# Keys and values of two batches turned at once, and scores as products of array halves, in a fused attention and expert kernel

## The chip, the core and the metric

The kernel runs on one core of a Trainium2 chip. The core has five engines that work side by side, each through its own list of instructions in order, and that meet through semaphores: TensorE (PE) for matrix products, VectorE (DVE) and ScalarE (ACT) for elementwise work, GpSimd (POOL), and SyncE (SP), which here only starts transfers. A PE product needs its stationary operand loaded into the array first; the profile lists these loads apart, as PEld. PE writes only to PSUM, which DVE and ACT read. Other data lie in SBUF, whose 128 partitions are the rows of every tile.

The metric is the time of one execution on the device in microseconds (us); lower is better.

## The reference

Attention with pooled keys and values, and then a mixture of experts that takes one expert for each row:

```python
batch, n_heads, seq, head_dim = (8, 8, 576, 64)      # q, k, v
k_p = k.reshape(B, H, Sp, pool, D).mean(axis=3)      # pool = 8, Sp = 72
v_p = v.reshape(B, H, Sp, pool, D).mean(axis=3)
scores = scale * np.matmul(q, k_p.transpose(0, 1, 3, 2))
attn = exp(scores - max) / sum
x = np.matmul(attn, v_p)                             # rows: 4608 x 512
# experts: argmax of x @ w_gate, at most `capacity` rows for each of 8,
# relu(x @ w1) @ w2, times the row's gate probability
```

## The kernel before

The attention stage takes the first 210 us or so of the span, the experts the rest. The change touches the attention stage alone.

**Pooling.** Batches go in pairs, p = 0 to 3. The 576 rows of k and v of a pair come in as three transfers each (`raw`, `load_third`), with (batch, head, group) on the 128 partitions: partition (b h g) holds the nine pooled rows of one group. GpSimd adds eight rows to one in a tree of three additions (`tree`, L348 to L352) into `kps[p]` and `vps[p]`, [128, 9, 64]. For pair 0 VectorE helps.

**Turning.** The pooled rows have to stand with head_dim on the partitions. `turned` (L374) does this for one batch b and one of k and v: five products with the pooled tile as the stationary operand and the 64 columns of the identity that pick batch b as the moving one, into one PSUM bank `pk` (L382). The first four take two pooled rows of 64 together, 128 columns; the fifth the ninth row alone, 64 columns. `natural` (L387) copies them out on ACT in two copies (even and odd rows, L391). For keys, `prep_k` does this twice, into `kbs[b % 2]`, [128, 2, 8 heads, 72]: partitions 0 to 63 get the keys in half 0, partitions 64 to 127 the same keys in half 1, and the other two quarters stay zero from the start. For values, `prep_v` copies once, and then multiplies with `wgi` (identity and gate weights, L409) into the bank `pv`, which VectorE spreads to `vbd` (L411, L413).

**Units.** The queries of a batch are done in units of 256 rows and four heads; units of a pair number nine (j = 0 to 8, with n = 9p + j): four of the even batch, one `tail` that holds the last 64 rows of both batches (j = 4), and four of the odd batch. `q_part` transposes two row blocks of one head together (L433), so that partitions 0 to 63 of `qT` hold the one block and 64 to 127 the other. `score` (L436) then multiplies `qT[:, h]`, stationary, with the 144 columns of `kbs` for that head: because of the zeros, one product over 128 rows gives the 72 scores of either block (L448). In a tail unit the stationary operand is the 64 columns of one batch, so that products come in pairs that fill the two column halves of the array (L445).

**Order.** It is written out by hand in the loop over n. PE's share of a step is: half of the scores of unit n (`score(0)`), half of the transposes of the probabilities of unit n - 2 (`p_t(0)`, L471), the other halves of both, the queries of unit n + 1 (L433), then the products with the values of unit n - 2 (`av`, L485). PSUM banks for all of PE's transposes are taken in turn from two (`bank`). `hooks(n)` at the end of a step adds the turning: `prep_k` of the odd batch at j = 1 and of the next pair's even batch at j = 5, `prep_v` at j = 2 and j = 6 with its second part (the product with `wgi`) one step later. SP runs the transfers of queries, keys and values in the order of the program.

An f32 product of the program is two load and product pairs in the trace, a transpose is one pair: `score` of two heads shows as x4, `av` as x12, `turned` as x10 (eight with 128 columns, two with 64).

Of the kernel before, what the change touches and what calls it, by code (L numbers as in the profile page):

```python
# [10 lines left out]
F32 = mybir.dt.float32  # L11
# [20 lines left out]
def pooled_attn_top1_moe(ctx: ExitStack, tc: tile.TileContext, q, k, v, wg, w1, w2, cap, out):  # L32
# [125 lines left out]
    with ExitStack() as actx:  # L158
# [85 lines left out]
        kbs = [ac.tile([P, 2, H, SP_], F32, name=f"kbs{i}") for i in range(2)]  # L244
# [6 lines left out]
        nc.vector.memset(kbs[0], 0.0)  # L251
# [122 lines left out]
        def turned(x, b, w):  # L374

            while left.get((w, b // 2)):
# [9 lines left out]
        def natural(dst, pk):  # L386

            v = dst.rearrange("d h (g r) -> d (h g) r", r=NR)
            for o in range(2):
                n = (NR + 1 - o) // 2  # L390
                nc.scalar.copy(v[:, :, o : NR : 2], pk[o * D : (o + 1) * D, 0 : n * GB].rearrange("d (i q) -> d q i", q=GB))  # L391

        def prep_k(b):

            ks = kbs[b % 2]
            pk = turned(kps[b // 2], b, "k")
            for x in range(2):
                natural(ks[x * D : (x + 1) * D, x], pk)

        def prep_v(b):  # L400

            vT = wk.tile([D, H, SP_], F32, name="vT", tag="vT", bufs=1)
            natural(vT, turned(vps[b // 2], b, "v"))
            yield
            vb = vbd[b % 2]
            rows_ = vT.rearrange("d h x -> d (h x)")
# [7 lines left out]
            yield  # L414

        class Unit:
# [19 lines left out]
            def score(self, part):  # L436
                if part == 0:
                    self.ps = psc.tile([P, HH, 256], F32, name="ps", tag="ps")
# [12 lines left out]
            def softmax(self):  # L451

                sv = self.ps[:, :, 0 : 2 * SP_].rearrange("p h (a x) -> p h a x", a=2)
# [220 lines left out]
        rq, hq, aq, dq, sq, gq = [], [], [], [], [], []  # L674
# [42 lines left out]
        with tc.manual_schedule():  # L717
            nc.gpsimd.memset(kbs[1], 0.0)
# [502 lines left out]
```

## Time and profile before

| | us |
|---|---|
| median of 3 runs | 669.99 (669.15 to 671.27) |
| profiled execution, its own time | 671.99 |
| its span, first to last instruction | 669.8 |
| PE busy, of the span | 625.5 (93%) |
| mean granted PE clock | 0.981 |

The profile is one execution; times in it count from the first instruction. A row of the order of time reads: start, length of the merged group (from its first start to its last end), engine, line, operation, tiles, shapes, count, and in brackets the idle time ahead of it with what ended it. Ends of PE products are modelled and overlap the next, so the distance from one row's start to the next row's start is the time that a group took. In shapes, 128*64 is the array's part used, rows by columns.

### The profile page before, as it was taken

To read this page: it belongs to the slowest core of one execution; us is meant where nothing else is said; L and a number is where in the kernel's file an instruction comes from. 1 tells how busy PE (TensorE), PEld (TensorE's weight loads), DVE (VectorE), ACT (ScalarE), POOL (GpSimd) and SP (SyncE) were. 2 spreads that over 40 slices of the span, in tenths; PEclk is the share of its full clock that TensorE was granted. 3 is DMA by queue.
4 is the path that set the end of the run, shared out by engine and by line. 5 is a ranking of instruction groups with operands and counts; after the bars stand their busy time and mean duration, and the time that the engine had idled before them with its cause. 6 is when DMAs were issued, how large, how long until landed. Compare 5 with 4: busy or idle time off the path is not lost. (4 is left out here: it accounts for less than half of the span.)

```text
span 669.8 us, 14743 instructions
## 1 busy us (share of the span) xinstructions
PE 625.5 (93%) x4218; PEld 560.6 (84%) x4219; DVE 343.9 (51%) x783; ACT 236.8 (35%) x401; POOL 310.6 (46%) x467
## 2 busy tenths in 40 slices
PE   2899989999878989999999999999999999999994
PEld 2899879888777878997888899897998978989983
DVE  4466767778778832227826642224622466221222
ACT  2455545556454111215616431124311463111111
POOL 7699952543386323135543444313543056431444
PEclk9799989999899989999999999999999999999998
DMA  9994844344273151014843761101711181110112
GB/s 326 372 385 138 322 158 127 126 155 145 81 244 120 47 192 31 31 63 171 325 152 142 252 253 63 31 31 63 289 63 31 35 300 38 63 31 31 63 47 64
DMA packets 47086, 93.82 MB, mean 140 GB/s; under 512 B 13392, under 2 KB 23632, under 8 KB 47060
## 3 DMA queue, kind: packets, MB, share of 16 engines
q1 hardware_dynamic: 30836, 60.37, 25.9%
q0 software_dynamic: 11392, 21.57, 9.8%
q10 hardware_dynamic: 4832, 11.56, 4.5%
q8 instruction: 13, 0.21, 0.1%
q14 instruction: 13, 0.11, 0.1%
HBM read 132.97 MB, written 31.27 MB: 245 GB/s over the span
## 5 line engine op out<-in xcount | busy, mean ns | idle before, releaser
L1132 ACT ACTIVATE hh<-ph 128x512 fp32r<-128x512 f32 x60 | 35.9, 599 | 181.3 <-PE ph L146 169.7
L1133 DVE SCALAR_TENSOR_TENSOR hl<-ph,hh 128x512 fp32r<-128x512 f32 x60 | 41.0, 691 | 110.8 <-ACT hh L1132 47.6
L146 PE MATMUL ph<-xl,w1h 128*128 128x256 f32 x480 | 76.8, 282 | 2.6 <-DVE io L86 2.6
L146 PE MATMUL ph<-xh,w1h 128*128 128x256 f32 x480 | 76.9, 282 | 2.1 <-DVEq L1158 2.1
L146 PE MATMUL ph<-xh,w1l 128*128 128x256 f32 x480 | 76.5, 281 | 0.0
L155 PE MATMUL y<-w2h,hh 128*128 128x512 f32 x280 | 72.3, 400 | 0.0
L155 PE MATMUL y<-w2h,hl 128*128 128x512 f32 x280 | 71.0, 396 | 0.0
L155 PE MATMUL y<-w2l,hh 128*128 128x512 f32 x280 | 71.0, 396 | 0.0
L146 PEld LDWEIGHTS ph<-xh,w1h 128*128 128x128 f32 x480 | 66.7, 190 | 3.8 <-issue 2.5
L91 POOL DMA_INDIRECT xg<-xs,ix x42 | 41.1, 978 | 61.8 <-PE y L155 52.3
L146 PEld LDWEIGHTS ph<-xl,w1h 128*128 128x128 f32 x480 | 65.4, 189 | 3.3 <-issue 3.3
L146 PEld LDWEIGHTS ph<-xh,w1l 128*128 128x128 f32 x480 | 65.5, 190 | 0.0
L485 PE MATMUL pa<-vbd,pT 96*128 96x146 f32 (+1 forms) x480 | 63.1, 296 | 1.7 <-DVE lt L511 1.5
L155 PEld LDWEIGHTS y<-w2h,hl 128*128 128x128 f32 x280 | 52.6, 188 | 12.7
L155 PEld LDWEIGHTS y<-w2l,hh 128*128 128x128 f32 x280 | 52.6, 188 | 12.7
L89 POOL TENSOR_TENSOR guard<-ix 128x4 int32<-128x4 int32 x21 | 4.1, 197 | 122.6 <-DVE ix L86 77.5
L485 PEld LDWEIGHTS pa<-vbd,pT 96*128 96x128 f32 (+1 forms) x480 | 58.0, 186 | 3.0 <-ACT pT L472 2.4
L155 PEld LDWEIGHTS y<-w2h,hh 128*128 128x128 f32 x280 | 50.0, 188 | 9.4
L1153 DVE TENSOR_SCALAR ys<-y,io 128x512 f32<-128x512 f32 x40 | 30.0, 751 | 48.9 <-PE y L155 43.7
L122 DVE TENSOR_TENSOR xl<-px,xh 128x512 fp32r<-128x512 f32 x40 | 25.7, 685 | 56.4 <-ACT xh L121 56.4
L96 POOL DMA_INDIRECT out_dram<-zrow,iz x40 | 47.4, 1184 | 14.8 <-issue 13.6
L472 ACT COPY pT<-pp 96x384 f32<-96x384 f32 x72 | 33.9, 475 | 45.3 <-PE pp L471 44.2
(256 smaller groups left out, 1095.0 us busy)
## 6 DMA issues: line engine op xcount, KB each, us to landing
r<-in_moe_w_dram SPq DMA_DIRECT2D x84, 1024.0 KB, 10.9
raw<-in_k_dram SPq DMA_DIRECT2D x12, 768.0 KB, 7.4
raw<-in_v_dram SPq DMA_DIRECT2D x12, 768.0 KB, 9.4
xs<-xo ACTq DMA_DIRECT2D x16, 512.0 KB, 2.8
qblk<-in_q_dram SPq DMA_DIRECT2D x14, 512.0 KB, 6.0
raw<-in_moe_w_dram SPq DMA_DIRECT2D x4, 512.0 KB, 5.2
r<-in_moe_w_dram ACTq DMA_DIRECT2D x2, 1024.0 KB, 8.5
qblk<-in_q_dram SPq DMA_DIRECT2D x4, 256.0 KB, 8.1
```

What stands on the lines that cost most here:

```text
L89: nc.gpsimd.tensor_sub(guard, ix, ix)
L91: nc.gpsimd.indirect_dma_start(out=dst[:, i, :].bitcast(F32), out_offset=None, in_=src, in_offset=bass.IndirectOffsetOnAxis(ap=ix[:, i, 0: ...
L96: ins = nc.gpsimd.indirect_dma_start(out=out[:, :], out_offset=bass.IndirectOffsetOnAxis(ap=i_, axis=0), in_=src, in_offset=None, bounds_c ...
L122: eng.tensor_sub(lo, src, hi.bitcast(F32))
L146: nc.tensor.matmul(p[:, f2], a[:, c, f * P : (f + 1) * P], b[:, c], start=(f2 == 0 and j == 0 and c == 0), stop=(f2 == 1 and j == 2 and c ...
L155: nc.tensor.matmul(y, a[:, c, i * P : (i + 1) * P], b[:, c], start=(n == 0), stop=(n == 3 * KF - 1))
L472: nc.scalar.copy(self.pT[:, j], pp[0:KC, 0:HC])
L485: nc.tensor.matmul(self.pa[us, j, h0 * XW : (h0 + 2) * XW], self.pT[:, j, c, us], vbd[b % 2][:, cc].rearrange("r a x -> r (a x)"), start=( ...
L1132: nc.scalar.activation(hh[s], p, AF.Relu)
L1133: nc.vector.scalar_tensor_tensor(out=hl[s], in0=p, scalar=0.0, in1=hh[s].bitcast(F32), op0=ALU.max, op1=ALU.subtract)
L1153: nc.vector.tensor_scalar_mul(ys[i], y[i], io[:, i, 1:2].bitcast(F32))
```

## The change

`turned` now handles both batches of a pair, with five PE transposes (the whole 128-column identity moving): four into bank `pk`, the ninth row into a second bank `pl`. Three ACT copies take them out: two of 64x512, one of 64x128. Keys go to `kTp[p % 2]`, [128, 16 heads, 72]: partitions 0 to 63 are copied by ACT, and partitions 64 to 127 are a copy of them by a transfer on SP's queue (for pair 0 by three more ACT copies). Values go to `vTp`. The zeros are gone, with the two fills that made them.

`score` issues, for each head, two products over 64 rows each, of 72 columns: rows 0 to 63 of `qT` with rows 0 to 63 of `kTp` into one PSUM bank, rows 64 to 127 into the next. In a tail unit it is four products of 64 rows and 64 columns of the array.

In the hooks, the keys of the next pair are turned at j = 4, its values at j = 5, and the products with `wgi` come at j = 2 and j = 7, in one piece.

```diff
-        def turned(x, b, w):
+        def turned(dst, x, w, p):
...
-            pk = bank([P, 512], "pk")
-            bs = slice((b % 2) * GB, (b % 2 + 1) * GB)
-            for i in range(0, NR, 2):
-                m = min(2, NR - i) * D
-                nc.tensor.matmul(pk[0:m, i // 2 * GB : (i // 2 + 1) * GB], x[:, i : min(i + 2, NR)].rearrange("p r d -> p (r d)"),
-                                 ident[:, bs], start=True, stop=True)
-            return pk
...
+            pk, pl = bank([P, 4, P], "pk"), bank([P, 512], "pl")
+            for i in range(NR // 2):
+                nc.tensor.transpose(pk[:, i], x[:, 2 * i : 2 * i + 2].rearrange("p r d -> p (r d)"), ident)
+            nc.tensor.transpose(pl[0:D, 0:P], x[:, NR - 1], ident)
+            for t in dst:
+                v = t.rearrange("d h (g r) -> d (h g) r", r=NR)
+                for o in range(2):
+                    nc.scalar.copy(v[:, :, o : NR - 1 : 2], pk[o * D : (o + 1) * D].rearrange("d i q -> d q i"))
+                nc.scalar.copy(v[:, :, NR - 1 :], pl[0:D, 0:P, None])
+
+        def prep_k(p):
+            kt = kTp[p % 2]
+            if p:
+                turned([kt[0:D]], kps[p], "k", p)
+                nc.sync.dma_start(kt[D:], kt[0:D])
+            else:
+                turned([kt[0:D], kt[D:]], kps[p], "k", p)
...
-                    if self.tail:
-                        for u, b in enumerate(self.bs):
-                            us = slice(u * TAIL, (u + 1) * TAIL)
-
-                            two = kbs[b % 2].rearrange("p a h x -> p (a h) x")[:, h : h + H + HH + 1 : H + HH]
-                            nc.tensor.matmul(self.ps[us, h, 0 : 2 * SP_].rearrange("p (a x) -> p a x", a=2), self.qT[:, h, us], two,
-                                             start=True, stop=True)
-                    else:
-                        nc.tensor.matmul(self.ps[:, h, 0 : 2 * SP_].rearrange("p (a x) -> p a x", a=2), self.qT[:, h],
-                                         kbs[self.b % 2][:, :, self.hf * HH + h], start=True, stop=True)
+                    x = slice(h * SP_, (h + 1) * SP_)
+                    for u, b in enumerate(self.bs):
+                        us = slice(u * TAIL, (u + 1) * TAIL) if self.tail else slice(0, P)
+                        for a in range(2):
+                            rs = slice(a * D, (a + 1) * D)
+                            hd = (b % 2) * H + h + HH * (a if self.tail else self.hf)
+                            nc.tensor.matmul(self.ps[us, a, x], self.qT[rs, h, us], kTp[b // 2 % 2][rs, hd], start=True, stop=True)
...
                 elif n == 1:
-                    hq.append(prep_v(0))
-                    drain(hq)
+                    turned([vTp], vps[0], "v", 0)
+                    prep_v(0)
                 if p == B // 2:
                     return
-                if j == 1:
-                    prep_k(2 * p + 1)
                 if j == 2:
-                    hq.append(prep_v(2 * p + 1))
+                    prep_v(2 * p + 1)
                 if p + 1 < B // 2:
+                    if j == 4:
+                        prep_k(p + 1)
                     if j == 5:
-                        prep_k(2 * p + 2)
-                    if j == 6:
-                        hq.append(prep_v(2 * p + 2))
+                        turned([vTp], vps[p + 1], "v", p + 1)
+                    if j == 7:
+                        prep_v(2 * p + 2)
```

**PE, before, in the second pair, from the products with the values of step j = 1 on.** Rows are line, operation, output and inputs, the output's partitions x columns, and how many of the program's instructions stand in a row (`kbs_143` and `vbd_146` are tile names with their numbers).

```order
L485 MATMUL pa<-vbd_146,pT 128x146 x6
L382 MATMUL pk<-identr,kp 128x64 x4
L382 MATMUL pk<-identr,kp 64x64
L448 MATMUL ps<-kbs_143,qT 128x144 x2
L471 MATMUL pp<-identr,pt 96x128 x3
L448 MATMUL ps<-kbs_143,qT 128x144 x2
L471 MATMUL pp<-identr,pt 96x128 x3
L433 MATMUL pq<-identr,qblk 128x128 x4
```

**PE, after, at j = 4 of the first pair,** where the keys of both batches of the second pair are turned:

```order
L475 MATMUL pa<-vbd_146,pT 128x146 x6
L380 MATMUL pk<-identr,kp 128x128 x4
L381 MATMUL pl<-identr,kp 64x128
L439 MATMUL ps<-kTp_143,qT 128x72 x4
L461 MATMUL pp<-identr,pt 96x128 x3
L439 MATMUL ps<-kTp_143,qT 128x72 x4
L461 MATMUL pp<-identr,pt 96x128 x3
L425 MATMUL pq<-identr,qblk 128x128 x4
```

The turning keeps its five instructions, but there is one such place for a pair where there were two; each group of scores has twice the instructions, each with half of the columns.

**PE, after, where the product with `wgi` stands ahead of scores,** at j = 7 of the second pair:

```order
L475 MATMUL pa<-vbd_147,pT 128x146 x6
L402 MATMUL pv<-wgi,vTp 96x80 x6
L439 MATMUL ps<-kTp_144,qT 128x72 x4
L461 MATMUL pp<-identr,pt 96x128 x3
L439 MATMUL ps<-kTp_144,qT 128x72 x4
```

Like the scores behind it, the product with `wgi` uses 64 rows of the array.

**SP, the transfers of the first pair's time.** Before:

```order
L204 DMA qblk<-in_q_dram 128x4x256 x2
L187 DMA raw<-in_k_dram 128x1536 x3
L187 DMA raw<-in_v_dram 128x1536 x3
L204 DMA qblk<-in_q_dram 128x4x256 x2
L212 DMA qtail<-in_q_dram 64x4x64 x4
```

After:

```order
L204 DMA qblk<-in_q_dram 128x4x256 x2
L392 DMA kTp_144<-kTp_144 64x1152
L187 DMA raw<-in_k_dram 128x1536 x3
L187 DMA raw<-in_v_dram 128x1536 x3
L204 DMA qblk<-in_q_dram 128x4x256 x2
L212 DMA qtail<-in_q_dram 64x4x64 x4
```

The copy of the keys to the lower partitions stands ahead of the loads of the third pair's keys and values.

## Rows read from the trace of the kernel before

**Rows 1.** Busy time of each engine in stretches of 20 us of the attention stage, with the granted PE clock: the stretch, its length, then busy us and instructions of PE, PEld, DVE, ACT and POOL, the clock as a share of full speed, the busy share of the DMA engines, GB/s.

```profile
100.00:120.00 20.00, 20.00 (x166) 19.06 (x165) 14.41 (x45) 11.13 (x22) 5.95 (x10) 1.00 0.35 107
160.00:180.00 20.00, 15.96 (x134) 14.25 (x133) 16.45 (x51) 11.61 (x25) 9.64 (x9) 0.99 0.17 54
```

**Rows 2.** What PE waited for from 16 to 240 us: total us, times, longest.

```profile
PE pp L471 <- DVE vbd L413: 4.0, 2, 2.0
...
PE pp L471 <- ACT kbs L391: 1.9, 6, 0.3
PE pq L433 <- ACT pT L472: 1.8, 2, 1.1
```

**Rows 3.** PE in order of time: one step without turning, and the start of the next.

```profile
63.11 0.65 PE L448 MATMUL ps<-kbs,qT 128*128 128x144 f32 x4
63.60 0.49 PE L471 MATMUL pp<-identr,pt 128*96 128x128 f32 x3
63.93 0.66 PE L448 MATMUL ps<-kbs,qT 128*128 128x144 f32 x4
...
64.75 0.62 PE L433 MATMUL pq<-identr,qblk 128*128 128x128 f32 x4
65.20 1.66 PE L485 MATMUL pa<-vbd,pT 96*128 96x146 f32 x12
66.70 0.66 PE L448 MATMUL ps<-kbs,qT 128*128 128x144 f32 x4
```

**Rows 4.** PE in order of time: a turning of keys, the step behind it, a turning of values, and the start of what follows its step.

```profile
70.29 1.26 PE L382 MATMUL pk<-identr,kp 128*128 128x64 f32 x10
71.48 0.76 PE L448 MATMUL ps<-kbs,qT 128*128 128x144 f32 x4
...
73.39 0.53 PE L471 MATMUL pp<-identr,pt 128*96 128x128 f32 x3 [0.33 <-ACT kbs L391]
...
75.88 1.26 PE L382 MATMUL pk<-identr,vp 128*128 128x64 f32 x10
...
80.86 1.24 PE L409 MATMUL pv<-wgi,vT 64*96 64x80 f32 x12
```

**Rows 5.** PE in order of time: full-row products, the product with `wgi` on 64 rows, full-row products again.

```profile
103.55 1.66 PE L485 MATMUL pa<-vbd,pT 96*128 96x146 f32 x12
105.14 1.24 PE L409 MATMUL pv<-wgi,vT 64*96 64x80 f32 x12
106.31 0.76 PE L448 MATMUL ps<-kbs,qT 128*128 128x144 f32 x4
106.91 0.49 PE L471 MATMUL pp<-identr,pt 128*96 128x128 f32 x3
```

**Rows 6.** PE in order of time: scores of a tail unit, on two column halves.

```profile
129.00 0.71 PE L445 MATMUL ps<-kbs,qT 128*64 128x144 f32 x8
129.64 0.53 PE L471 MATMUL pp<-identr,pt 128*96 128x128 f32 x3
130.10 0.71 PE L445 MATMUL ps<-kbs,qT 128*64 128x144 f32 x8
```

**Rows 7.** PE in order of time: the router's counts, products of 8 columns that each load 128 columns, and the turning behind them.

```profile
99.64 0.37 PE L604 MATMUL po<-su,rlow 128*128 128x8 f32 x2
99.86 0.37 PE L604 MATMUL po<-su,chigh 128*128 128x8 f32 x2
100.08 1.34 PE L382 MATMUL pk<-identr,vp 128*128 128x64 f32 x10
```

**Rows 8.** ACT's copies out of PSUM from 16 to 240 us, by shape: count, busy us, mean ns of one, idle ahead.

```profile
L434 ACT COPY qT<-pq 128x512 f32<-128x512 f32 x36 | 21.1, 586 | 7.6 <-PE pq L433 6.7
L391 ACT COPY kbs<-pk 64x320 f32<-64x320 f32 x14 | 6.1, 437 | 8.8 <-PE pk L382 8.7
L391 ACT COPY kbs<-pk 64x256 f32<-64x256 f32 x14 | 5.8, 414 | 0.2
```

**Rows 9.** PE in order of time, at the start.

```profile
16.05 2.29 PE L448 MATMUL ps<-kbs,qT 128*128 128x144 f32 x8 [1.38 <-ACT qT L434]
...
24.21 1.24 PE L409 MATMUL pv<-wgi,vT 64*96 64x80 f32 x12 [1.56 <-ACT vT L391]
25.38 1.96 PE L382 MATMUL pk<-identr,kp 128*128 128x64 f32 x10
27.27 1.33 PE L448 MATMUL ps<-kbs,qT 128*128 128x144 f32 x4
```

**Rows 10.** PE in order of time, in the fourth batch pair's first steps.

```profile
163.60 0.53 PE L471 MATMUL pp<-identr,pt 128*96 128x128 f32 x3 [0.32 <-ACT kbs L391]
165.26 0.66 PE L433 MATMUL pq<-identr,qblk 128*128 128x128 f32 x4 [1.13 <-ACT pT L472]
```

**Rows 11.** Busy time and granted clock of two neighbouring stretches, around a wait of PE (columns as in rows 1).

```profile
83.90:87.30 3.40, 1.45 (x13) 1.48 (x14) 3.40 (x9) 0.90 (x2) 3.24 (x4) 1.00 0.66 210
87.30:90.70 3.40, 3.40 (x16) 3.35 (x16) 1.76 (x7) 0.85 (x2) 3.24 (x4) 0.50 1.01 349
```

**Rows 12.** GpSimd in order of time: the last addition for the second pair's values and the first for the third pair's keys.

```profile
45.95 0.59 POOL L352 TENSOR_TENSOR vp<-t 128x192 f32<-128x192 f32 x1
...
53.36 1.80 POOL L348 TENSOR_TENSOR t<-raw 128x768 f32<-128x768 f32 x1
```

**Rows 13.** SP's queue in order of time: the issue of the loads of the third pair's keys.

```profile
32.76 2.04 SPq L187 DMA_DIRECT2D raw<-in_k_dram  x3
```

More of the change, by code (lines that the diff above doesn't have):

```diff
@@ L241, in pooled_attn_top1_moe @@
                                     wg.rearrange("(h d) e -> d h e", d=D)[:, h0 : h0 + HC])
-        kbs = [ac.tile([P, 2, H, SP_], F32, name=f"kbs{i}") for i in range(2)]
+        kTp = [ac.tile([P, 2 * H, SP_], F32, name=f"kTp{i}") for i in range(2)]
+        vTp = ac.tile([D, 2 * H, SP_], F32, name="vTp")
         vbd = [ac.tile([KC, NCH, 2, XW], F32, name=f"vbd{i}") for i in range(2)]
@@ L372, in pool @@
                     gq.append(tree(dst[:, third(i)], raws[p]["kv".index(w)][i], (w, p)))
-        def turned(x, b, w):
-            while left.get((w, b // 2)):
+        def turned(dst, x, w, p):
+            while left.get((w, p)):
                 step(gq)
-            pk = bank([P, 512], "pk")
-            bs = slice((b % 2) * GB, (b % 2 + 1) * GB)
-            for i in range(0, NR, 2):
-                m = min(2, NR - i) * D
-                nc.tensor.matmul(pk[0:m, i // 2 * GB : (i // 2 + 1) * GB], x[:, i : min(i + 2, NR)].rearrange("p r d -> p (r d)"),
-                                 ident[:, bs], start=True, stop=True)
-            return pk
@@ L386, in natural @@
[L386 to L398, printed above, removed]
+            pk, pl = bank([P, 4, P], "pk"), bank([P, 512], "pl")
@@ L400, in prep_v @@
+        def prep_k(p):
[5 more added lines that the diff above has]
+                turned([kt[0:D], kt[D:]], kps[p], "k", p)
         def prep_v(b):
-            vT = wk.tile([D, H, SP_], F32, name="vT", tag="vT", bufs=1)
-            natural(vT, turned(vps[b // 2], b, "v"))
-            yield
             vb = vbd[b % 2]
-            rows_ = vT.rearrange("d h x -> d (h x)")
+            rows_ = vTp[:, (b % 2) * H : (b % 2 + 1) * H].rearrange("d h x -> d (h x)")
@@ L413, in prep_v @@
             nc.vector.tensor_mul(vb[:, :, :, 0:D], pv[:, :, None, 0:D].to_broadcast([KC, NCH, 2, D]), m.to_broadcast([KC, NCH, 2, D]))
-            yield
         class Unit:
@@ L437, in score @@
                 if part == 0:
-                    self.ps = psc.tile([P, HH, 256], F32, name="ps", tag="ps")
+                    self.ps = psc.tile([P, HH, 256], F32, name="ps", tag="ps").rearrange("p (a h) x -> p a (h x)", a=2)
                 for h in range(part * HH // 2, (part + 1) * HH // 2):
-                    if self.tail:
-                        for u, b in enumerate(self.bs):
-                            us = slice(u * TAIL, (u + 1) * TAIL)
-                            two = kbs[b % 2].rearrange("p a h x -> p (a h) x")[:, h : h + H + HH + 1 : H + HH]
-                            nc.tensor.matmul(self.ps[us, h, 0 : 2 * SP_].rearrange("p (a x) -> p a x", a=2), self.qT[:, h, us], two,
-                                             start=True, stop=True)
-                    else:
-                        nc.tensor.matmul(self.ps[:, h, 0 : 2 * SP_].rearrange("p (a x) -> p a x", a=2), self.qT[:, h],
-                                         kbs[self.b % 2][:, :, self.hf * HH + h], start=True, stop=True)
+                    x = slice(h * SP_, (h + 1) * SP_)
[5 more added lines that the diff above has]
+                            nc.tensor.matmul(self.ps[us, a, x], self.qT[rs, h, us], kTp[b // 2 % 2][rs, hd], start=True, stop=True)
             def softmax(self):
-                sv = self.ps[:, :, 0 : 2 * SP_].rearrange("p h (a x) -> p h a x", a=2)
+                sv = self.ps[:, :, 0 : HH * SP_].rearrange("p a (h x) -> p h a x", x=SP_)
                 mx = sm.tile([P, HH, 2], F32, name="mx", tag="mx")
@@ L673, in pooled_attn_top1_moe @@
                 units += [Unit(b, i, hf) for hf in range(2) for i in range(NB // 2)]
-        rq, hq, aq, dq, sq, gq = [], [], [], [], [], []
+        rq, aq, dq, sq, gq = [], [], [], [], []
         def route_of(u):
@@ L717, in pooled_attn_top1_moe @@
         with tc.manual_schedule():
-            nc.gpsimd.memset(kbs[1], 0.0)
             rest = setup()
@@ L1033, in hooks @@
                         pool(p + 2)
-                step(hq)
                 if n == NB:
```

1 line of the change is left out of this document (removed).

## The prediction, on record before the changed kernel ran

> **What bounds the kernel now.** I read the busy time by stretches first. From 100 to 120 us PE is busy for all of 20 us at full clock, and DVE for 14.4 [rows 1]: in the attention stage PE sets the pace, and PE time that goes or comes moves the end. From 160 to 180 us PE is busy for 16.0 and DVE for 16.5 [rows 1]; there the two wait for each other, which is a rival below. Then PE's own waits: the largest, 4.0 us in two waits, is for VectorE's spreading of `pv`, and 1.9 us go to the key copies on ACT [rows 2]. So this is a sum of PE time, and I take it from distances between starts in order of time. A step without turning takes 66.70 - 63.11 = 3.59 us; a half of the scores in it 0.49, that half with its three transposes 0.82, a transpose 0.45 / 4 = 0.11 [rows 3].
>
> **Removed: the turnings.** A turning of keys costs 75.88 - 70.29 - 3.59 = 2.00 us, of which some 0.6 is the wait of the next transposes for the copies on ACT and what restarts behind it; one of values costs 80.86 - 75.88 - 3.59 = 1.39 [rows 4]. In the stream there are six of keys at 2.00, one near the start at 27.27 - 25.38 = 1.89 [rows 9], and seven of values at 1.39: 23.6 us in all, besides the first of each.
>
> **Added: six turnings of a pair.** Four transposes of 0.11 make 0.44. The ninth row uses 64 columns, so the array changes its division: entering another division costs 1.59 against 1.50 us from the start of `av` to the next group, 0.09 [rows 3, 5]; with 0.05 for a load that nothing hides (estimate, half of a 128-column load) and 0.11 for the transpose this is 0.69. Both PSUM banks are taken, and the next transposes need the first one back. ACT copies it out in two copies of 64x512; the copy of 128x512 takes 0.59, so I take 0.59 each [rows 8]; 64x128 lies under the 0.41 of 64x256, and I take 0.3 [rows 8]. With 0.65 until the transposes are out, the bank is free 1.9 us after the start; PE comes back for it after 0.69 and a half of scores, at 1.4. Wait: 0.5, between 0.3 and 0.8. A turning: 1.2 us. Six: 7.2, and the balance of the turnings is **-16.4 us** (-18 to -14.5).
>
> **Scores, the price of halves.** Nothing in the trace shows products in the lower 64 rows, so I bound them. What is seen: a tail unit's eight pairs with 64 columns each, in two column halves, take 129.64 - 129.00 = 0.64 us, and with the transposes 1.10 [rows 6]. Eight pairs of 0.12 one behind another would take 0.98; so the two halves work side by side, as four pairs, 0.49, and the rest, 1.10 - 0.82 = 0.28, is what it costs to go into another division and back. A load of 128 columns sets the pace where the product is short: two such pairs every 0.22 us, 0.11 each, whatever their 8 columns [rows 7]. The new products have 72 columns, half of today's 0.12, 0.06, so the load binds, and halving the rows halves no load: 12 pairs of `wgi` with 64 rows and 96 columns take 1.17, 0.10 each [rows 5].
>
> Now a half of the scores (two heads) has eight pairs, four in the upper rows and four in the lower. If the two rows of pairs run side by side: 4 x 0.112 + 0.28 = 0.73 against 0.49, +0.24. If one behind another: 8 x 0.112 + 0.28 = 1.18, +0.69. I take the first, since its nearest row is the tail unit, in which halves of the array that meet no common columns do overlap, loads too. The Trainium skill, "TensorE: Matmul & The Clock Gate", section "Part 3: Packing small matmuls — row/col tiling", says that loads overlap products in flight only in other row groups, and that products in different row groups run at the same time; by it the first price holds, by its opposite the second. The trace shows this for columns [rows 6] and no run here yet for rows.
>
> There are 64 halves: 32 units that are not tails. 52 at +0.24: +12.5. Eight stand behind a product with `wgi`, which uses 64 rows as well: the way in, half of 0.28, falls away, and 0.73 - 0.14 = 0.59 meets today's 0.60 [rows 5]; the way out of that product, another 0.09, goes too: -0.10 each, -0.8. The four of the first two units have no transposes between them and run at the lower clock; 16 pairs side by side are 0.90 + 0.28 against 0.98 a unit, half as much again for the clock: +0.6 together. **Scores: +12.3 us** (+10 to +15 if side by side).
>
> **Tails.** Eight halves with 16 pairs of 64 columns in four quarters: four loads or products of about 0.06 and 0.28 make 0.53, against 0.49 + 0.28 = 0.77 [rows 6]. -0.24 each, **-1.9** (0 if only two quarters overlap).
>
> **The start.** Keys of pair 0 need six copies: 4 x 0.59 + 2 x 0.3 = 2.96 against 4 x 0.43 [rows 8]. PE stands for ACT there now [rows 9], so +1.2 (+0.5 at least, since fewer pairs follow the last arrival). The first values take three copies, 1.5 against 0.85, in a wait of PE for them [rows 9]: +0.65. **+1.9.** The two fills of zeros run before the first data arrive; nothing for them.
>
> **Late waits.** In the fourth pair PE waits 1.13 us for a copy on ACT [rows 10], behind key copies that are now gone: **-1.0** (0 to -1.2).
>
> **What moves, at no cost.** The turnings come one or more steps earlier, and need GpSimd's sums sooner. The second pair's last sum is done at 45.95 + 0.59 = 46.5 us [rows 12]; its values are turned at n = 5, which comes at about 49 by the terms above (today 47.35, less 1.9 and 1.4, plus 1.9, 1.2 and six steps of 0.4). Cover of 2 us; if it fails, PE waits what is missing once. SP's new transfer waits for ACT at n = 4, some 46 us, and the third pair's loads, issued from 32.8 us today [rows 13], wait behind it; they take some 8 us to land, and GpSimd wants the first at 53.4 [rows 12]: perhaps 1 us late for work that is not due before 90 us. The lower half of the keys has four steps, 15 us, to arrive. Behind it on SP stand only loads.
>
> **Sum.** -16.4 + 12.3 - 1.9 + 1.9 - 1.0 = -5.1 us. The profiled execution took 671.99, so its like would take 666.9; the median is 2.0 lower, and against 669.99 this gives **665.0 us**, with 661 to 669 from the bounds that belong to this case.
>
> **Rivals.** *One behind another (slower).* The two row halves share the way by which stationary operands come in, and loads queue: 52 x 0.69 + 8 x 0.35 + 3 (start) = +41.7 in place of +12.3, tails 0: +26, **696 us**. It decides from the point at which a half of the scores takes over 0.8 us. Against it: the column halves load side by side [rows 6]. For it: they read different columns, and these would read into the same ones.
>
> *The clock falls more often.* From 83.9 to 87.3 us PE was busy for 1.45 of 3.40, and for the next 3.4 us the clock was 0.50, its lower level, 1.2 GHz: 1.7 us lost [rows 11]. A turning now brings 3.8 us between two `av` groups in which PE changes its division, waits and runs short products. If it falls after all six: +10, **675**; after three, 670, no change. Against it: the turnings of today, as load-bound, ran at full clock [rows 4].
>
> *VectorE takes the gain.* Where DVE is as busy as PE [rows 1], the last pair's two turnings (3.4 us) would be given back as waits for DVE: **668.4**, no change.
>
> *The full factor.* The Trainium skill, "TensorEngine Tiling (Array Packing)", section "Overview", gives up to twice the speed for a dimension of 64 or less. As a mechanism here, loads and changes of division would hide behind other work, and a half of the scores would take 0.25 in place of 0.49: 64 x -0.24 = -15.7 in place of +12.3, **637 us**. The loads at 0.11 [rows 7] and the 0.28 [rows 6] speak against it.
>
> **Chances.** Forecast 0.58, one behind another 0.13, the clock 0.15, VectorE 0.11, full factor 0.03. A run of this kernel can be told from no change beyond 0.3%, 2 us. Faster: 0.54 of the forecast's, and 0.03: 0.57. Slower: 0.13, half of the clock's, and a little: 0.22. Same: 0.21. The range takes in the forecast's bounds, VectorE, and the clock up to all six turnings: 659.5 to 676; the serial case and the full factor stay out, with some edges, about 0.2.
>
> **What would show it.** Right: groups of scores 0.7 us from start to start, the products of both row halves beginning within some ns; six turnings of about 1.2 us; steps without turning at about 4.07 instead of 3.59. Wrong: a half of the scores of 1.1 us or more (serial); a granted clock under 1.00 between 100 and 160 us (clock); a PE wait for DVE of 2 us in new places.

## The result and the profile of the changed kernel

The changed kernel took 677.02 us (median of 20 runs, 670.46 to 684.84) against 670.76 (20 runs, 668.42 to 675.45): a ratio of 1.0064 with an interval of 1.0036 to 1.0092. It is slower by 0.6%, where 665.0 was forecast, and its median lies one us outside the range. (Ratios here and below leave out runs that took over 1.5% more than the fastest of their kernel, so they differ a little from those of the medians; the profiled executions of the changed kernel and of e8 are two such runs.) The profiled execution took 681.59 us, its span 679.4, at a mean granted clock of 0.973.

**What came out as worked out.** PE in order of time, a step without turning and the start of the next two (answers rows 3):

```profile
69.54 0.67 PE L439 MATMUL ps<-kTp,qT 64*128 64x72 f32 x8
70.14 0.53 PE L461 MATMUL pp<-identr,pt 128*96 128x128 f32 x3
...
73.60 0.67 PE L439 MATMUL ps<-kTp,qT 64*128 64x72 f32 x8
...
77.66 0.56 PE L439 MATMUL ps<-kTp,qT 64*128 64x72 f32 x6
```

Eight pairs of 64 rows take 0.60 us until the transposes start; one behind another their loads alone would be 8 x 0.112 = 0.90. The row halves do run side by side. A step is 73.60 - 69.54 = 4.06 us, forecast 4.07, before 3.59 [rows 3]. The tails, in the same view (answers rows 6):

```profile
87.69 0.48 PE L439 MATMUL ps<-kTp,qT 64*64 64x72 f32 x16
88.10 0.53 PE L461 MATMUL pp<-identr,pt 128*96 128x128 f32 x3
88.56 0.48 PE L439 MATMUL ps<-kTp,qT 64*64 64x72 f32 x16
```

A half takes 88.56 - 87.69 = 0.87 with its transposes, against 1.10 [rows 6]: -0.23, forecast -0.24.

**The turnings.** PE in order of time, one of keys and one of values (answers rows 4):

```profile
49.36 0.60 PE L380 MATMUL pk<-identr,kp 128*128 128x128 f32 x4
...
51.40 0.53 PE L461 MATMUL pp<-identr,pt 128*96 128x128 f32 x3 [0.73 <-ACT kTp L385]
...
54.77 0.60 PE L380 MATMUL pk<-identr,vp 128*128 128x128 f32 x4
...
58.77 1.72 PE L475 MATMUL pa<-vbd,pT 96*64 96x146 f32 x24
60.42 0.67 PE L439 MATMUL ps<-kTp,qT 64*128 64x72 f32 x8
```

54.77 - 49.36 - 4.06 = 1.35 us for keys and 60.42 - 54.77 - 4.06 = 1.59 for values, forecast 1.2. Of the 1.59, 0.15 is not the turning's: the `av` of this step is the tail unit's, on 64 columns, and takes 60.42 - 58.77 = 1.65 us instead of 1.50 [rows 3]; the kernel before has it too. So a turning of values costs 1.44. The wait is 0.73 instead of 0.5: ACT's copies of 64x512 took 0.67 each, not 0.59 (ACT's copies by shape, answers rows 8):

```profile
L385 ACT COPY vTp<-pk 64x512 f32<-64x512 f32 x8 | 5.3, 669 | 2.9 <-PE pk L380 2.9
```

**PE's waits** from 16 to 240 us (answers rows 2):

```profile
PE pp L461 <- DVE vbd L406: 4.4, 2, 3.5
PE pp L461 <- ACT kTp L385: 3.5, 3, 2.1
PE pq L425 <- ACT kTp L385: 3.0, 1, 3.0
...
PE pv L402 <- ACT vTp L386: 1.8, 1, 1.8
```

(L406 is the spread, L385 and L386 are ACT's copies, L425 are the queries.) The third is the start: `pk` and `pl` hold both banks, so already the first queries wait for six copies. First scores and first values, in order of time (answers rows 9):

```profile
16.11 1.11 PE L425 MATMUL pq<-identr,qblk 128*128 128x128 f32 x4 [2.99 <-ACT kTp L385]
17.89 1.99 PE L439 MATMUL ps<-kTp,qT 64*128 64x72 f32 x16 [0.68 <-ACT qT L426]
...
27.60 2.05 PE L402 MATMUL pv<-wgi,vTp 64*96 64x80 f32 x11 [1.81 <-ACT vTp L386]
...
33.97 3.13 PE L475 MATMUL pa<-vbd,pT 96*128 96x146 f32 x12
```

The first scores start 1.84 us later than before [rows 9]. `av` at 33.97 takes 3.13 us instead of 1.66 [rows 3]: the lower clock. It lasted until 45.0 us here, and until 32.7 before (with full clock from 19.1 to 25.9).

**The two waits that matter.** The profiles of e6 and e13, the same kernel again, show both as well: 2.26 and 3.50 us, 2.10 and 3.50. First the key copies of the third pair, in order of time, DVE:

```profile
90.46 1.56 DVE L581 TENSOR_TENSOR su<-gwi,goh 128x8 f32<-128x8 f32 x1
91.94 0.74 DVE L450 TENSOR_TENSOR pt<-ps,mx 128x576 f32<-128x576 f32 x1
```

GpSimd there:

```profile
90.17 1.82 POOL L348 TENSOR_TENSOR t<-raw 128x768 f32<-128x768 f32 x1
```

ACT:

```profile
92.72 0.68 ACT L453 ACTIVATE pt<-pt 128x576 f32<-128x576 f32 x1 [2.10 <-DVE pt L450]
93.31 1.34 ACT L385 COPY kTp<-pk 64x512 f32<-64x512 f32 x2
```

And PE:

```profile
94.70 0.53 PE L461 MATMUL pp<-identr,pt 128*96 128x128 f32 x3 [2.12 <-ACT kTp L385]
```

Read it upwards. PE waits for ACT's copies; these stand behind the exponential; that waits for DVE's subtraction `pt`; and ahead of this DVE has a tiny addition of the router (8 columns) that takes 1.56 us and ends at 92.02, with GpSimd's addition (90.17 + 1.82 = 91.99). Otherwise these additions take 0.16 us, as the first row of the next place shows, the step with the last batch's spread (DVE):

```profile
170.02 0.16 DVE L581 TENSOR_TENSOR gwi<-goh 128x8 f32<-128x8 f32 x1
...
170.83 3.07 DVE L581 TENSOR_TENSOR gwi<-goh 128x8 f32<-128x8 f32 x1
173.82 0.68 DVE L500 TENSOR_TENSOR xo<-pa,rz 128x512 f32<-128x512 f32 x1
...
174.80 0.94 DVE L406 TENSOR_TENSOR vbd<-pv,mk 96x768 f32<-96x768 f32 x1
```

GpSimd, its subtractions for the experts' weights:

```profile
171.38 2.49 POOL L122 TENSOR_TENSOR w1l<-raw,w1h 128x512 fp32r<-128x512 f32 x2
```

PE:

```profile
175.88 0.84 PE L461 MATMUL pp<-identr,pt 128*96 128x128 f32 x3 [3.52 <-DVE vbd L406]
```

The addition ends at 173.90, GpSimd's two subtractions at 173.87. The spread of `pv` stands behind it on DVE, and PE's next transposes need the bank that `pv` holds. The Trainium skill, "SBUF — State Buffer", section "Terms", says that VectorE and GpSimd arbitrate for one pair of ports, and that the loser blocks while the other's instruction lasts. The equal ends agree with it; no run here takes GpSimd's operation away. They are no accident of two rows: in the twenty profiles, 125 copies and additions of 128x8 on VectorE in the first 235 us took over 0.7 us, and each of them ended 20 to 34 ns after an operation of GpSimd.

Behind each of the two waits the clock falls (granted clock of stretches, columns as in rows 1; answers rows 11):

```profile
96.20:99.60 3.40, 3.40 (x16) 3.40 (x15) 1.28 (x3) 1.65 (x3) 2.74 (x3) 0.50 0.47 114
174.70:188.40 13.70, 12.52 (x82) 11.83 (x82) 7.41 (x32) 4.94 (x10) 2.50 (x2) 0.50 0.09 38
```

The kernel before has the same thing ahead of both of its waits of 2.0 us for a spread, of which the prediction says only that they are for the spread [rows 2]. VectorE, before, in order of time:

```profile
81.57 1.74 DVE L591 TENSOR_TENSOR gwi<-goh 128x8 f32<-128x8 f32 x1
...
84.76 0.94 DVE L413 TENSOR_TENSOR vbd<-pv,mk 96x768 f32<-96x768 f32 x1
...
175.04 1.17 DVE L626 COPY gps<-gba 128x8 f32<-128x8 f32 x1
...
177.71 0.94 DVE L413 TENSOR_TENSOR vbd<-pv,mk 96x768 f32<-96x768 f32 x1
```

The addition and the copy end 28 and 29 ns after an operation of GpSimd. So the waits for spreads did not appear with the change: they grew at one place, from 1.96 to 3.52 us, and shrank at the other, from 2.01 to 0.85. What is new is the wait of 2.12 for the key copies, where the profile of the kernel before has none over 0.33.

### The profile page after: what moved, and what is told of

Same layout as the page of the kernel before. It is cut to its first block, busy times and chain, and to the rows that moved or that the text cites. A ratio compares the mean times of both kernels' runs of the same rounds, so it can differ in the third digit from the quotient of the medians.

```text
span 679.4 us, 15097 instructions
## 1 busy us (share of the span) xinstructions
PE 629.9 (93%) x4418; PEld 557.2 (82%) x4419; DVE 341.9 (50%) x782; ACT 231.9 (34%) x380; POOL 309.4 (46%) x466
## 5 line engine op out<-in xcount | busy, mean ns | idle before, releaser
L1120 ACT ACTIVATE hh<-ph 128x512 fp32r<-128x512 f32 x60 | 35.9, 599 | 182.7 <-PE ph L146 179.1
L475 PE MATMUL pa<-vbd,pT 96*128 96x146 f32 (+1 forms) x480 | 67.2, 308 | 1.0 <-DVE lt L501 0.8
L475 PEld LDWEIGHTS pa<-vbd,pT 96*128 96x128 f32 (+1 forms) x480 | 62.7, 198 | 2.2 <-ACT pT L462 1.5
L96 POOL DMA_INDIRECT out_dram<-zrow,iz x40 | 47.5, 1187 | 14.8 <-issue 13.5
```

What stands on the lines that cost most here:

```text
L96: ins = nc.gpsimd.indirect_dma_start(out=out[:, :], out_offset=bass.IndirectOffsetOnAxis(ap=i_, axis=0), in_=src, in_offset=None, bounds_c ...
L475: nc.tensor.matmul(self.pa[us, j, h0 * XW : (h0 + 2) * XW], self.pT[:, j, c, us], vbd[b % 2][:, cc].rearrange("r a x -> r (a x)"), start=( ...
L1120: nc.scalar.activation(hh[s], p, AF.Relu)
```

## The experiments

All are timed against the kernel before in their own session. The sessions differ: its median was 678.5 (e1 to e4), 679.6 (e5 to e8), 670.8 (e9 to e12), 670.7 (e13 to e16) and 670.1 us (e17, e18). *Low time* is (1 - mean granted clock) x 2 x span, mean over the runs that the ratio counts: the time at the lower clock after its first rise. *Stage* is the time from the first to the fourth tail unit's scores in the profiled execution; by the prediction's terms it should shrink by 6.0 us (12 turnings -20.3, six new +7.2, halves +9.5, tails -1.4, late waits -1.0).

| run | ratio to before | low time | stage |
|---|---|---|---|
| before | 1 | 15.8 to 26.6 by session | 135.3 |
| changed | 1.0064 (1.0036 to 1.0092) | 34.2 | 136.2 |
| e1 turning alone | 0.9894 (0.9860 to 0.9929) | 26.1 | 131.2 |
| e2 scores alone | 1.0162 (1.0116 to 1.0208) | 35.9 | 139.6 |
| e3 changed, filled start | 1.0063 (1.0024 to 1.0103) | 50.9 | 142.0 |
| e4 before, filled start | 0.9964 (0.9935 to 0.9992) | 25.9 | 135.1 |
| e5 before again | one run | 23.0 | 134.0 |
| e6 changed again | 1.0106 (1.0064 to 1.0148) | 42.5 | 143.0 |
| e7 as e3 | 1.0064 (1.0026 to 1.0102) | 53.5 | 139.3 |
| e8 scores in one piece | 1.0040 (1.0002 to 1.0078) | 46.1 | 132.9 |
| e9 as e1 | 0.9888 (0.9844 to 0.9932) | 26.1 | 130.8 |
| e10 e1, padded | 1.0063 (1.0030 to 1.0096) | 25.5 | 136.2 |
| e11 changed, padded | 1.0312 (1.0278 to 1.0346) | 32.0 | 144.9 |
| e12 e1, filled start | 0.9878 (0.9844 to 0.9913) | 28.0 | 131.3 |
| e13 changed again | 1.0046 (1.0011 to 1.0081) | 28.4 | 137.9 |
| e14 changed, router held | 1.0151 (1.0109 to 1.0194) | 42.6 | 136.0 |
| e15 e1, router held | 1.0024 (0.9995 to 1.0054) | 35.2 | 131.9 |
| e16 e12, router held | 0.9982 (0.9952 to 1.0013) | 37.7 | 136.6 |
| e17 changed, two places | 0.9967 (0.9939 to 0.9995) | 23.7 | 125.7 |
| e18 e1, two places | 0.9863 (0.9837 to 0.9889) | 26.1 | 122.8 |

**e1 and e2: each half of the change by itself.** e1 keeps the zeros and the full-row scores, fed by the new turning (to make room for the zeros, one small tile shares another's place); e2 keeps the old turning and writes the keys of both partition halves for 64-row scores.

```diff
 e1, against the changed kernel:
-            turned([kt[0:D], kt[D:]], kps[p], "k", p)
+            turned([kt[0:D, 0], kt[D:, 1]], kps[p], "k", p)
...
-            nc.tensor.matmul(self.ps[us, a, x], self.qT[rs, h, us], kTp[b // 2 % 2][rs, hd], start=True, stop=True)
+            nc.tensor.matmul(self.ps[:, h, 0 : 2 * SP_].rearrange("p (a x) -> p a x", a=2), self.qT[:, h],
+                             kTp[self.b // 2 % 2][:, :, (self.b % 2) * H + self.hf * HH + h], start=True, stop=True)
 e2, against the kernel before (its scores are those of the changed one):
-            ks = kbs[b % 2]
+            ks = kTp[b // 2 % 2][:, (b % 2) * H : (b % 2 + 1) * H]
-                natural(ks[x * D : (x + 1) * D, x], pk)
+                natural(ks[x * D : (x + 1) * D], pk)
```

> The new turning (a pair of batches at once, the same places in the loop) with the old scores: full-row products with zeros in the keys. If the loss of the change is the clock's, and the clock stays low at the start because products on 64 rows do not bring it up (theory B), this kernel has full clock from about 20 us on, as before, and comes out at -16 for turnings and +3 for the start: 656 to 660 us, 0.98 of before. If the clock stays low because PE stands longer at the start for ACT's six key copies (theory A), transposes last 0.21 us each until some 45 us here as well, about 9 us are lost, and it is 664 to 669 us. If the new turning itself saves nothing (theory C, the sum was wrong), 670 or more.

> The old turning (each batch by itself) with the new scores. The sum of PE time gives +12.3 for scores and -1.9 for tails: 680 us at the same clock as before (theory A: the start is as before, transposes at 0.11 us from some 33 us on). Theory B (products on 64 rows do not bring the clock up): transposes at 0.21 us until 45 us or longer, 686 to 690 us. Steps without turning last 4.06 us in both.

Neither theory came out whole. Applied to 670 us, the time of the kernel before that the bounds take, the ratios make 663 us for e1 and 681 for e2, nearest to theory A in both; the clock's last rise at the start, at 32.8 us in e1 and at 45.4 in e2, is what theory B said.

The two add up within their intervals: -1.06% + 1.62% = +0.56%, the change +0.64%. The turning gives some 7 us, where the prediction counted 15.5 (-16.4 + 1.9 - 1.0); the scores cost some 11 by the ratio, where it counted 10.4. So what is missing is, for the most part, half of the turnings' gain.

**e3, e4 and e7: filled start.** The lower clock of the first 45 us was my first suspect. Products of the identity with itself, into a bank that nobody reads yet, fill PE's waits of the first 28 us.

```diff
+        def fill(n):
+            for _ in range(n):
+                nc.tensor.matmul(dummy[0][:, 0, 0:P], ident, ident, start=True, stop=True, skip_group_check=True)
```

> The changed kernel with 27 products of identity by identity (128 rows, 128 columns) put into PE's waits of the first 28 us, into a PSUM bank that nobody reads. Theory A: the clock comes up by 10 to 12 us and stays; the first tail's scores start at 38 to 40 us instead of 45.8, and the time falls by 6 to 9 us against the changed kernel, to 666 to 670. Theory B: the clock comes up for the filler and falls again among the 64-row products, gain 1 to 4 us. If the clock has no part in it, the added work costs 1 to 3 us.

> The kernel before with 22 such products in its waits of the first 25 us. Its transposes last 0.21 us before 19 us and from 26 to 33 us; with the clock up all along it gains 3 to 5 us, 666 to 668 us. Without effect of the filler on the clock, 670 to 672.

> The changed kernel with filler products in PE's waits of the first 28 us, now beside the changed kernel itself. Theory A/B (the clock at the start is the loss): first tail's scores 6 to 8 us earlier, and the time 5 to 8 us under the changed kernel's. Rival (VectorE and later waits take back what PE gains early): first tail as early, but the time within 2 us of the changed kernel's.

The clock rose at 8 to 12 us and the first tail unit came at 38.2 and 37.8 us (e3, e7) instead of 45.8 and 40.8 (changed, e6). Little of it reached the end, and e7 against e6, 0.4%, lies between its two theories: the lead is used up by the router's waits and a lower clock behind them, in e7 27 us of it from 196 to 223 us.

**e5, e6 and e8: the same again, and scores in one piece.** e5 and e6 are unchanged. e8 puts the first transposes ahead of both halves of the scores (behind both in the steps that follow a turning), so that the scores stand in one piece; this spares one of two changes of division.

```diff
+                late = (n - 1) % NPU in (4, 5) and n < 3 * NPU
+                if p and not late:
+                    p.p_t(0)
                 if u:
                     u.score(0)
-                if p:
+                    u.score(1)
+                if p and late:
                     p.p_t(0)
...
-                    u.score(1)
```

> The kernel before, for its trace on the chip of the next three, since the sum compares traces of one chip. Theory B (scores on 64 rows keep the clock low at the start): full clock, transposes of 0.11 us, by some 33 us. All theories expect its tail units to start at about 40, 82, 129 and 175 us after the first instruction.

> The changed kernel once more, beside the next two on one chip: 1.003 to 1.010 of before in all theories. Theory B: where its trace has transposes of 0.21 us until some 45 us, its first tail's scores start 5 to 6 us later than those of the kernel before on this chip.

> The changed kernel with both halves of a step's scores in one piece, between the two groups of transposes: one change of the array's division there and back for a step instead of two. If a change there and back costs 0.28 us, a step without turning or product with wgi falls from 4.06 to 3.78 us, some 20 of them, and the six turning steps lose about 0.5 us each: -7 to -9 us against the changed kernel. If the price is not in the change of division but in the loads, no step changes by more than 0.1 us. Rival (VectorE takes it): steps shorten in the first three pairs, the time by less than 3 us.

A step of e8 takes 72.43 - 68.66 = 3.77 us (its transposes' starts) against 4.06: the way in and out of the other division costs 0.29, forecast 0.28. Its stage, 132.9, is 10 us shorter than that of e6, but its median is only 5 us lower, less than the 7 to 9 expected. e6 shows the clock up at 25.4 us for a while, so 45 us is not fixed.

**e9 to e12: 64 rows or longer steps?** e10 and e11 add one full-row product behind each half of the scores, into columns that nobody reads; e12 is e1 with the filler.

```diff
+                nc.tensor.matmul(self.ps[:, part * HH // 2, 2 * SP_ : 256], ident, ident[:, 0 : 256 - 2 * SP_], start=True, stop=True)
```

> The new turning of a pair with the old full-row scores, a second time, beside its two variants. Whatever the theory: 0.985 to 0.993 of the kernel before. The mean granted clock gives the time at the lower level after the first change, (1 - clock) x 2 x time: in all runs so far 24 to 27 us where scores are full-row products (mean clock 0.980 to 0.982) and 36 to 54 us where they are 64-row products (0.960 to 0.973). Theory that the 64-row products bring the clock down: 25 to 28 us here. Rival, that the turnings and their waits do: over 33.

> As e9, with one more full-row product (identity by 112 columns, into columns that nobody reads) behind each half of the scores, so that a half of the scores takes about as long as in the changed kernel: 64 times 0.22 to 0.24 = 14 to 15 us of PE more, a step of about 4.05. It tells 64 rows from longer steps. Theory that 64-row products bring the clock down: low time stays at 24 to 30 us, and the time is that of e9 plus 8 to 15 us (some of it hidden in the late stage). Rival, that longer steps shift the balance between PE, ACT and DVE, and the waits that come of it bring the clock down: low time of 36 us or more, as in the changed kernel, time that of e9 plus 18 or more.

> The changed kernel with the same full-row product behind each half of its 64-row scores: 14 to 15 us of PE more, a step of about 4.5. If the lower clock comes from how much of PE's time goes to 64-row products, the low time falls from some 43 us to 33 or less, and the time is 1.015 to 1.025 of before. If 64-row products bring it whatever stands beside them, low time stays over 38 us and the time is 1.028 or more.

> e9 with the filler products of the first 28 us, that is both parts that helped by themselves (0.989 and 0.996). If they add up: 0.984 to 0.988. If the late stage takes the lead of the start, as it did with the changed kernel: as e9, 0.987 to 0.992. First change of the clock at 8 to 12 us instead of some 26 to 36, fourth tail unit at 166 to 170 us.

e10 has steps of 3.99 us and loses no more to the clock than e9: longer steps are not the cause. Of its 64 x 0.21 = 13.4 us of added PE work, 10.1 show in the median (674.95 - 664.84) and 11.7 by the ratios: PE time that comes moves the end by three quarters of itself or more. e11's low time of 32.0 us is what the share of full-row work foretold, its time what the opposite did; it doesn't decide. e12 adds nothing to e9 that can be told apart. At this point I held the 64-row products for the cause of the low time; e17 speaks against it.

**e13 to e16: the router held back.** The small additions are the router's. In steps that turn or spread they are left to the end of the step.

```diff
+        def route_step(n):
+            if held[0]:
+                held[1] += n
+            else:
+                step(rq, n)
...
+                held[0] = held[0] or (u is not None and n % NPU in (2, 4, 5, 7))
...
                 hooks(n)
+                if n % NPU != 4:
+                    held[0] = False
+                    route_step(held[1])
+                    held[1] = 0
```

> The changed kernel once more, as the partner of e14 on the same chip: 1.004 to 1.012 of before. Its trace should show the two waits again: some 2 us of the transposes for the key copies near 90 to 95 us, and some 3.5 us for VectorE's spread ahead of the fourth tail unit, each behind a small VectorE addition of 1.5 to 3.1 us (0.16 by itself) that ends with an operation of GpSimd.

> The changed kernel with the router's small VectorE operations held back in the steps that turn or spread (j = 2, 4, 5 and 7) and issued behind them; nothing else is moved but the router's own products. Theory that part of the loss is these additions, held by GpSimd's operations on the same tiles' memory, with the copies and the spread queued behind them, and the lower clock after PE's long waits: the waits of 2.1 and 3.5 us fall under 1.0 each, the stretch at the lower clock behind each is gone or shorter, the fourth tail unit starts 3 to 6 us earlier than in e13, and the time is 2 to 5 us below e13. Rival, that these waits are the last pair's VectorE load as such (VectorE as busy as PE): the 3.5 us only moves to the next step, and the time stays within 1.5 us of e13.

> The new turning with the old full-row scores, and the router held back as in e14. The same theory: its wait of 3.1 us for the spread falls under 1.0, and the time is 0.983 to 0.987 of before (0.989 without). Rival: 0.988 to 0.990. If the turnings then give most of what the prediction counted for them (15.5 us less some 3 for their larger waits), the time would be 0.981 or less.

> As e15, with the filler products of the first 28 us (e12 without the holding: 0.988). By the theory 0.981 to 0.986; by the rival as e12.

A miss by its edit. e14's stage is 1.9 us shorter than e13's and the wait of 3.5 us is gone. The wait for the key copies stayed, at 2.18: there an addition of the step ahead, at 84.31, took 1.57 us. And the edit also held the router where nothing is turned, and its products then came right behind the additions that feed them (PE in e14, in order of time):

```profile
175.47 0.59 PE L594 MATMUL po<-su,upper 128*128 128x24 f32 x2 [2.80 <-DVE su L590]
...
192.89 0.57 PE L594 MATMUL po<-su,upper 128*128 128x8 f32 x2 [4.89 <-DVE gci L596]
```

The time was 1.0% over e13's; e15 and e16 missed too (1.0024 and 0.9982, where 0.983 to 0.987 and 0.981 to 0.986 were expected). It showed that the wait for the spread is the router's doing, and not what it is worth.

**e17 and e18: two places only.** The router skips two steps, n = 13 and n = 29, and goes on in the next, so that its products come a step later.

```diff
+        def route_step(n):
+            if not held[0]:
+                step(rq, n)
...
+                held[0] = n in (13, 29)
```

> The changed kernel with the router's VectorE operations left out of two steps only (n = 13 and n = 29, where the waits of 2.1 and 3.5 us stand) and done from the next step on, so that its products come one step later, without the bursts that gave e14 new waits of 4.9 and 2.8 us. Theory of the held additions: both waits fall under 1.0 us, no wait over 2 us appears in their place before 182 us, the fourth tail unit starts 3 to 6 us after the first one less than in e13 (137.9 us between them in e13, so 132 to 135), and the time is 0.996 to 1.003 of before. Rival, that the last pair's VectorE work bounds as such: the wait comes back in the next step, 136 us or more between the tail units, and 1.004 to 1.011 as in the three runs without it.

> The same in the kernel with the new turning and the old full-row scores (0.9894 and 0.9888 without it, 130.8 to 131.2 us between the first and the fourth tail unit). Theory of the held additions: 0.980 to 0.986, 126 to 129 us between the tail units. Rival: 0.987 to 0.991, 130 or more.

What PE waited for in e13 from 84 to 180 us, that is from the second tail unit to the fourth:

```profile
PE pp L461 <- DVE vbd L406: 3.5, 1, 3.5
PE pp L461 <- ACT kTp L385: 2.7, 2, 2.1
PE pp L461 <- ACT vTp L385: 1.5, 2, 0.7
```

The same in e17, from 83 to 176 us, some way past the fourth:

```profile
PE pa L475 <- DVE lt L501: 1.9, 1, 1.9
PE pp L461 <- ACT vTp L385: 1.5, 2, 0.7
PE pp L461 <- ACT kTp L385: 1.5, 2, 0.8
```

In e17 the spread comes ahead of the additions, and the wait for it is gone; the additions are still held, one step later, and cost one wait of 1.9. DVE of e17 in order of time:

```profile
163.54 0.94 DVE L406 TENSOR_TENSOR vbd<-pv,mk 96x768 f32<-96x768 f32 x1
...
167.95 1.15 DVE L581 TENSOR_TENSOR su<-gwi,goh 128x8 f32<-128x8 f32 x1
```

PE of e17, the key copies of the third pair and the late wait:

```profile
89.10 0.53 PE L461 MATMUL pp<-identr,pt 128*96 128x128 f32 x3 [0.84 <-ACT kTp L385]
...
171.34 2.62 PE L475 MATMUL pa<-vbd,pT 96*128 96x146 f32 x12 [1.93 <-DVE lt L501]
```

The stage shrinks from 137.9 to 125.7 us, and the ratio from 1.0046 (1.0064 and 1.0106 in the other runs) to 0.9967: the theory of the held additions came out, with more of the stage gone than it expected. Of the 12.2 us, 4.8 are the two waits, and some 6.4 the lower clock, which in e13 lasts from 91.1 to 98.0 and from 173.1 to 183.3 us. Not all of it is gained: behind the wait of 1.9, and so behind the end of the stage, e17's clock is at its lower level from 172.1 to 182.3 us, and its median is 7 us below e13's. The low time is 23.7 us, that of full-row scores. With these two places mended the changed kernel is 0.3% faster than the one before, by an interval that ends just short of 1. e18, at 0.9863, can't be told from e9 at 0.9888 by its time, though its stage is 8 us shorter; its median, 661.32 us, is the lowest of this study. What the same edit would give the kernel before, which has waits of this kind for both of its spreads, was not run.

## Why the prediction was wrong

It forecast -5.1 us; the medians say +6.3. **The step that failed is "What moves, at no cost".** It asked whether GpSimd's sums and SP's transfers would be in time for the earlier turnings (they were: PE waits for neither in the attention stage; the cover of 2 us is 3 by its own terms, which add up to 49.6 and not 49), and left out VectorE's queue. The change moves the last spread one step ahead, to a step in which the router's additions stand ahead of it, and the keys' turning to where their copies stand behind an exponential that waits for such an addition. "PE sets the pace, so PE time that goes moves the end" then failed at these two places. e17 shows their worth: 0.8% or 5 us against e13, 1.4% or 9 us against e6, by the ratios. How much of that is the change's own loss is open, since the wait for the last spread was there before, shorter, and no run takes the router's additions out of the kernel before.

Between the first and the fourth tail unit of the profiled executions, -6.0 was forecast and +0.9 came. The turnings cost 9.7 in place of 7.2: three of keys at 1.35, 2.74 (with the wait of 2.12) and 1.24, three of values at 1.44. The waits for spreads are 4.4 against 2.0, since the last one, which before comes behind the fourth tail unit, now comes ahead of it. A wait of 0.6 for ACT went that nobody had counted. The clock was at its lower level for 10.6 us of it against 3.4; in 1.2 of these PE still stood, and half of the rest is lost: +3.0. Together +2.5 + 2.4 - 0.6 + 3.0 = 7.3, close to the 6.9 that are to be explained.

**Removed and added turnings.** The mechanism was right, the size of the wait at 0.5 was not: 0.73 even where nothing is late, since 64x512 costs ACT 0.67. "Both banks are taken" was seen for the steps and missed at the start, where it makes the 2.99 us wait. The first scores came 1.84 us later, where +1.2 was forecast, and the wait for the first values grew from 1.56 to 1.81, +0.25 where +0.65 was forecast; that the two add up to 2.1, near the forecast 1.9, is luck.

**Scores and tails.** Right in every part: 4.06 for 4.07, side by side, tails -0.23. By the ratios they cost +1.04% from e18 to e17, 7.0 us, and +1.62% in e2, 11.0, against +10.4 forecast; the intervals do not tell the two apart. The rule of the Trainium skill, "TensorE: Matmul & The Clock Gate", section "Part 3: Packing small matmuls — row/col tiling", that products in different row groups run at the same time and loads overlap there, agrees with the 0.60.

**Late waits.** Right: the wait of 1.13 us [rows 10] is gone. But the last wait for a spread is longer by 1.6 us.

**The rivals.** One behind another and the full factor are refuted by the step of 4.06. "The clock falls more often" happened, and at 675 was the nearest price: low time is 28.4 against 17.4 us for the kernel before in the session of e13, and 42.5 against 23.5 in that of e6, half of which is lost. But in the profile of the changed kernel 17.1 us of it lie behind the two long waits, and none behind the short work of the other turnings: the rival's sign, a clock under 1.00 between 100 and 160 us, is not in the profile of the changed kernel or of e13, and e17 keeps all six turnings and has a low time of 23.7. In e6 the clock did fall there, from 138.1 to 144.9 us, at the turning of the fourth pair's keys, behind no wait over 0.9 us; so the rival is not refuted there. "VectorE takes the gain" was right in its place, the last pair, and its sign, a PE wait for DVE of 2 us in a new place, is the wait of 3.52 (before it was 1.96, behind the tail unit's first scores); it was wrong in its reason: e17 has all of VectorE's work and the stage is 9.6 us shorter than before.

**What stays open.** The clock's last rise at the start is at 35.3 to 45.4 us in seven profiles with 64-row scores, and at 31.4 to 35.9 in six with full-row scores (none with filler or padding); the first tail unit comes at 40.8 to 47.5 and 38.1 to 42.9. So the clock seems to come up later there with the 64-row scores, and the tail unit some 3 us later in the medians, which the forecast lacks; but in e6 it rose at 25.4 and fell again, and nothing here says what decides it. e2's low time of 35.9 without a new turning is not explained either, nor why the kernel before differs by up to 9.5 us from session to session.

## What to carry to other kernels

When work moves by a step, go through the queue of every engine that serves it, not only of those that wait: what now stands ahead of a copy or a spread counts as much as its length. A tiny VectorE operation is worth looking up where it overlaps GpSimd's; if it ends when GpSimd's does, keep it away from what PE needs next. And sum gains of PE at less than their size: of PE time added at every step, three quarters or more reached the end here (e10), and of the 15.5 us that the turnings were to give, 7.2 and 7.5 (e1, e9), or 9.2 with the two waits gone (e18), figures that their intervals do not tell apart.

## What the runs showed of the hardware

A VectorE addition of 8 columns takes 0.16 us, and 1.56 or 3.07 us beside GpSimd's additions and subtractions; it then ends 20 to 34 ns after GpSimd's operation (125 cases over 0.7 us, copies included), in the longest case after the second of two. f32 products of 64 rows and 72 columns in both row halves start some ns apart, and eight take 0.60 us with one way into that division; entering and leaving it costs 0.29 a time. ACT's copy of 64x512 took 0.67 us, longer than its copy of 128x512 (0.59 [rows 8]).
